# Both filters of the first batch on two queues behind x, in fewer transfers, with the angle work on VectorE

## Chip, cores, metric

The kernel runs on one core of a Trainium2 chip. The metric is the device time of one execution in microseconds (us); lower is better. The profile comes from one execution; its span is about 2 us shorter than the time of the same execution (802.4 against 804.15 us for the kernel before).

Engines are TensorE (PE in the profile, PEld its weight loads), VectorE (DVE), ScalarE (ACT), GpSimd (POOL) and the sync engine (SP). Each of the last three can issue DMA transfers into a queue of its own: in the profile q0 is GpSimd's queue, q1 the sync engine's, q10 ScalarE's. All queues are served by the core's 16 DMA engines.

## The reference

```python
batch, seq, dim = (8, 3008, 256)          # x; filters have seq // 2 + 1 = 1505 rows
X = np.fft.rfft(x, axis=1)
y = np.fft.irfft(X * (filt_r + 1j * filt_i)[None], n=3008, axis=1)
h = y.reshape(24064, 256) @ w_in          # 256 -> 2048
g = h * (1.0 / (1.0 + np.exp(-beta * h)))
out = g @ w_out                           # 2048 -> 256
```

## The kernel before

The transform of length 3008 is cut into 47 x 64 and done as matmuls against tables of sines and cosines. The first batch is transformed alone, since nothing else can run yet: load `x`, first stage (`first1`), turn (`turn_a`), then twelve steps `product(i)` that multiply the spectrum by the real filter and by the imaginary one, each followed by `inverse3`, and a last stage. After it begins the long part, which I call the expert phase: 752 steps (47 blocks of 512 tokens times 16) of the two expert matmuls, among which the other seven batches are transformed. The first matmul of `hps` marks its beginning, and it comes up again and again below as "the first expert matmul".

Both filters live in one tile, `fr_sb`: partitions 0 to 63 hold the real one, 64 to 127 the imaginary one. Each group of a filter takes two transfers, the straight half and a mirrored half whose rows are read backwards.

```python
    def load_x(b, n):
        t = xpool.tile([NP, J, D], BF16, name="xg", tag="xg")
        xv = x[b].rearrange("(p j) d -> p j d", j=J)
        for g in range(n):
            js = slice(g * J // n, (g + 1) * J // n)
            nc.gpsimd.dma_start(t[:80, js, :], xv[:80, js, :])
            nc.gpsimd.dma_start(t[80:NP, js, :], xv[80:NP, js, :])
        return t

    def load_filter(f_sb, filt, at, k0, n, eng, later=False):
        lo = AP(filt.tensor, filt.offset + k0 * D, [[N1 * D, H], [1, n * D]])        # straight
        hi = AP(filt.tensor, filt.offset + (N1 - k0) * D, [[N1 * D, H], [-D, n], [1, D]])  # mirrored
        # ... (one transfer each into f_sb[at:at+H] and f_sb[at+H:at+M])

    # ... (iota, constants)
    x_cur = load_x(0, NJG)                                  # GpSimd's queue
    mark = dpool.tile([1, D], BF16, name="mark", tag="mark")
    nc.sync.dma_start(mark[:], x_cur[:1, 2 * JG, :])        # holds the sync queue until x is there
    for g in range(NG):                                     # NG = 4
        load_filter(fr_sb, filt_r, 0, g * KG, KG, nc.sync)  # real filter
    ws = [load_wout(i * WG, WG) for i in range(2)]          # output weights, sync queue
    # ... keep mask on GpSimd, tables
    angles(0, nc.vector)
    angles(1, gp)                                           # second half of the angles on GpSimd
    for g in range(NG):
        load_filter(fr_sb, filt_i, M, g * KG, KG, gp)       # imaginary filter, GpSimd's queue
    WI = 4
    # ... input weights: WI transfers on GpSimd's queue
    # ... first stage; turn

    for i in range(NK // 2 + 1):
        if i < NK // 2:
            product(i)
        # ... turns, tables, beta
        if i > 0:
            inverse3(i - 1)
    xs[1] = load_x(1, 2)                                    # x of the second batch
```

## Time and profile before

The time before is 803.57 us, the median of 3 runs (802.89 to 804.30).

| Stage of the kernel before | from, to (us) |
|---|---|
| loads, first stage, turn | 0 to 26.2 (first multiply of product 0) |
| product loop (first to last product's multiply) | 26.2 to 43.0 |
| last stage | 43.0 to 48.99 (first expert matmul) |
| expert phase | 48.99 to 802.4 |

The windows view gives the busy time of each engine in a stretch. Its columns are named in its first line; PEclk is the granted clock of TensorE, and a DMA share over 1 means that the records of the engines' packets overlap.

```profile
core 0: us, PE busy (x) PEld busy (x) DVE busy (x) ACT busy (x) POOL busy (x), PEclk, DMA share, GB/s
20.00:30.00 10.00, 5.88 (x49) 4.81 (x48) 4.16 (x8) 4.96 (x10) 3.19 (x6) 0.67 1.07 249
30.00:40.00 10.00, 9.91 (x127) 8.92 (x126) 8.75 (x18) 8.39 (x13) 4.03 (x9) 0.88 1.13 197
...
120.00:780.00 660.00, 658.76 (x5094) 465.76 (x5092) 318.79 (x495) 498.00 (x751) 96.81 (x82) 1.00 0.38 105
```

From 120 us on TensorE is busy 658.8 of 660 us at full clock, so the change has to earn its time before that (or in the last microseconds). There TensorE is idle 4.1 of the 10 us from 20 to 30, and the clock falls to 0.67, while the DMA engines are full.

The timeline shows start, duration, instruction, and in brackets how long the engine sat idle before it and what ended that.

```profile
25.75 0.35 DVE L373 TENSOR_SCALAR fr_sb<-fr_sb,keep 64x256 f32<-64x256 f32 x1 [6.96 <-DMA fr_sb<-in_filt_i_dram]
26.20 0.69 DVE L414 TENSOR_TENSOR pb_t<-ps,fr_sb 128x512 bf16<-128x512 f32 x1
...
43.03 0.68 DVE L414 TENSOR_TENSOR pb_t<-ps,fr_sb 128x512 bf16<-128x512 f32 x1
...
48.99 1.02 PE L735 MATMUL hps<-y,win_sb 128*128 128x512 bf16 x4
```

VectorE waits 6.96 us for the imaginary filter. The chain of waits (start, duration, what) says why that filter is late:

```profile
9.52 1.44 POOL u L257
...
11.04 2.82 POOL r L263
...
13.93 1.80 POOL u L264
...
16.32 9.30 DMA fr_sb<-in_filt_i_dram
```

GpSimd computes its half of the angles (9.5 to 15.7 us) before it issues the imaginary filter, whose second transfer then takes 9.30 us to land.

The third view counts what the queues moved in a window: packets, MB, and the time of those packets as a share of 16 engines. This is the kernel before from 12.5 to 20 us:

```profile
q1 hardware_dynamic: 1165, 1.62, 105.9%
q0 software_dynamic: 3, 0.00, 0.3%
```

A second window of the same kernel, 22 to 28 us, could have been read before predicting too. Both queues have work there, q0 in packets of 4,096 and 6,144 bytes and q1 in packets of 1,024:

```profile
q0 software_dynamic: 315, 1.06, 75.8%
q1 hardware_dynamic: 314, 0.32, 27.8%
```

The numbers of packets are equal and the bytes are not.

### The profile page before, as it was taken

How to read it: one execution, taken by the hardware profiler on the slowest of the kernel's cores; microseconds unless marked ns; L12 is line 12 of the kernel's file. 1: busy time of each engine (PE TensorE's matmuls, PEld its weight loads, DVE VectorE, ACT ScalarE, POOL GpSimd, SP SyncE). 2: the span in 40 equal slices, each digit the busy share in tenths (PEclk: the TensorE clock that was granted, in tenths of full speed). 3: DMA queues.
4: the chain of work that ended last, by engine and by line, in shares of the span. 5: the costliest groups of instructions: out<-in, count | busy, mean ns of one | idle time of the engine just before them, and what ended most of it. 6: DMA issues, size and time to landing. Idle time of an engine off the chain costs nothing.

```text
span 802.4 us, 15376 instructions
## 1 busy us (share of the span) xinstructions
PE 781.1 (97%) x6101; PEld 550.6 (69%) x6101; DVE 411.2 (51%) x665; ACT 588.6 (73%) x896; POOL 154.5 (19%) x157
## 2 busy tenths in 40 slices
PE   6799999999999999999999999999999999999997
PEld 3666667776677666776678766787666776776664
DVE  7676965574627645374653656347462670500101
ACT  4665787787677876788667886678767788677775
POOL 9370520231003400033001410023100240000000
PEclk9799999999999999999999999999999999999999
DMA  8989369322932158211780119602290124110101
GB/s 165 225 180 242 74 163 231 110 93 91 222 120 74 66 140 189 110 48 66 184 228 27 67 56 217 186 27 92 87 243 28 61 79 119 32 54 28 54 27 52
DMA packets 85058, 91.44 MB, mean 114 GB/s; under 512 B 3713, under 2 KB 76178, under 8 KB 84170
## 3 DMA queue, kind: packets, MB, share of 16 engines
q1 hardware_dynamic: 80250, 72.37, 30.5%
q0 software_dynamic: 3072, 14.94, 9.9%
q10 hardware_dynamic: 1664, 3.15, 2.0%
q8 instruction: 47, 0.77, 0.4%
q14 instruction: 25, 0.20, 0.1%
HBM read 57.16 MB, written 46.66 MB: 129 GB/s over the span
## 4 chain that ended last, share of the span: by engine, by line
PE 88%; DVE 4%; DMA 3%; POOL 2%; issue 2%; ACT 1%; DVEq 0%; POOLq 0%; SPq 0%; ACTq 0%
PE acc L763 39%; PE hps L735 38%; PE ps L541 3%; PE ps L489 2%; PE ps L563 2%; PE ps L590 2%; DMA d<-a 1%; DVE ost L775 1%; DMA fr_sb<-in_filt_i_dram 1%; PE psz L424 1%; DVE p_t L573 1%; DVE q_t L577 0%; DVE fi_sb L657 0%; DMA a<-d 0%; PE pz L481 0%
## 5 line engine op out<-in xcount | busy, mean ns | idle before, releaser
L744 ACT ACTIVATE gT<-hps,beta_sb 128x512 bf16<-128x512 f32 x752 | 516.0, 687 | 186.3 <-PE hps L735 173.9
L763 PE MATMUL acc<-wout_sb,gT 128*128 128x256 bf16 x3008 | 455.3, 272 | 2.4 <-DVE ost L775 1.3
L735 PE MATMUL hps<-y,win_sb 128*128 128x512 bf16 (+7 forms) x1728 | 447.6, 351 | 0.0
L763 PEld LDWEIGHTS <-gT 128*128 128x128 bf16 x3008 | 285.7, 98 | 134.2 <-issue 6.2
L735 PEld LDWEIGHTS <-win_sb 128*128 128x128 bf16 x1728 | 164.7, 98 | 24.5 <-issue 0.3
L580 POOL TENSOR_TENSOR v_t<-p_t,q_t 128x512 bf16<-128x512 f32 x84 | 106.6, 1269 | 377.5 <-DVE q_t L577 373.3
L775 DVE COPY ost<-acc 128x512 f32<-128x512 f32 x94 | 60.4, 683 | 193.7 <-PE acc L763 193.7
L107 DVE CAST a<-ps 96x512 bf16<-96x512 f32 x104 | 70.8, 686 | 81.8 <-PE ps L541 81.5
L109 DVE TENSOR_SCALAR y<-ps 128x376 bf16<-128x376 f32 x122 | 66.6, 548 | 65.5 <-PE ps L489 65.2
L573 DVE TENSOR_TENSOR p_t<-ps,fr_sb 128x512 f32<-128x512 f32 x84 | 58.1, 692 | 29.0 <-PE ps L563 27.5
L577 DVE TENSOR_TENSOR q_t<-ps,fi_sb 64x512 f32<-64x512 f32 x84 | 58.3, 694 | 1.2
L574 DVE SCALAR_TENSOR_TENSOR q_t<-ps,fi_sb 64x512 f32<-64x512 f32 x84 | 57.4, 683 | 1.1
L489 PEld LDWEIGHTS <-zz 96*128 96x128 bf16 x512 | 35.5, 98 | 29.1 <-issue 0.2
L105 ACT ACTIVATE z<-ps 128x512 bf16<-128x512 f32 x84 | 49.4, 588 | 1.0 <-PE ps L590 1.0
L541 PE MATMUL ps<-xg,t 94*96 94x512 bf16 x112 | 42.0, 381 | 0.5 <-DVE a L107 0.4
L489 PE MATMUL ps<-t,zz 96*128 96x94 bf16 x448 | 36.8, 205 | 0.0
L590 PE MATMUL ps<-v_t,t 128*128 128x256 bf16 x168 | 32.1, 273 | 0.7 <-DVE q_t L577 0.7
L563 PE MATMUL ps<-a,t 128*128 128x256 bf16 x168 | 32.1, 273 | 0.3 <-DMA a<-d 0.3
L116 POOL DMA_DIRECT2D xg<-in_x_dram x12 | 7.0, 584 | 116.2 <-PE acc L763 97.8
L563 PEld LDWEIGHTS <-t 128*128 128x128 bf16 x168 | 15.8, 98 | 14.8 <-issue 0.4
L541 PEld LDWEIGHTS <-t 94*96 94x96 bf16 x112 | 13.8, 123 | 12.6 <-issue 0.6
L590 PEld LDWEIGHTS <-t 128*128 128x128 bf16 x168 | 15.5, 98 | 8.5 <-DVE q_t L577 1.2
(115 smaller groups left out, 212.5 us busy)
## 6 DMA issues: line engine op xcount, KB each, us to landing
out_dram<-ost SPq DMA_DIRECT2D x41, 512.0 KB, 2.9
d<-a SPq DMA_DIRECT2D x28, 384.0 KB, 7.2
a<-d SPq DMA_DIRECT2D x28, 384.0 KB, 4.4
d<-z SPq DMA_DIRECT2D x28, 384.0 KB, 3.0
zz<-d SPq DMA_DIRECT2D x28, 384.0 KB, 5.1
xg<-in_x_dram POOLq DMA_DIRECT2D x6, 1280.0 KB, 10.2
out_dram<-ost SPq DMA_DIRECT2D x20, 128.0 KB, 3.6
ws<-in_moe_w_out_dram SPq DMA_DIRECT2D x4, 512.0 KB, 17.2
```

The costliest lines, as they stand in the source:

```text
L107: nc.vector.tensor_copy(dst, src)
L109: nc.vector.tensor_scalar_mul(dst, src, scale)
L489: nc.tensor.matmul(ps[:, e, :NP], lhsT=zz[:, jj + e, dc * P : (dc + 1) * P], rhs=tab[:], start=True, stop=True,)
L541: nc.tensor.matmul(ps[:KP], lhsT=t1[:], rhs=s["x"][:, 2 * i : 2 * i + 2, :], start=True, stop=True)
L563: nc.tensor.matmul(ps[:, e, :], lhsT=t2[:, k0 + e, 3:5, :].rearrange("p c k -> p (c k)"), rhs=s["a2"][g][:, kk + e, :], start=True, stop=True,
L573: nc.vector.tensor_tensor(p_t[:], ps[:], fr_sb[:, k0 : k0 + 2, :], ALU.mult)
L580: nc.gpsimd.tensor_tensor(v_t[:], p_t[:], q_t[:], ALU.add)
L590: nc.tensor.matmul(ps[:, e, :], lhsT=t3[:, k0 + e, :], rhs=v_t[:, e, :], start=True, stop=True)
L735: nc.tensor.matmul(hps[:, pos - t0 : pos - t0 + ln], lhsT=win_sb[:, dc, fb * P : (fb + 1) * P], rhs=ys[b][:, dc, n0 : n0 + ln], start=(dc ...
L744: nc.scalar.activation(gT[:, :tn], hps[:, :tn], ACT.Silu, scale=beta_sb[:, fb : fb + 1])
L763: nc.tensor.matmul(acc[tb // 2][:, tb % 2, :], lhsT=gT[:, tb * P : (tb + 1) * P], rhs=wout_sb[:, fb, :], start=(fb == 0 and tb % 2 == 0), ...
L775: nc.vector.tensor_copy(ost[:, 2 * h : 2 * h + n, :], acc[h][:, :n, :])
```

## The change

The intent is to end the 7 us wait. The imaginary filter is issued right behind `x`, before any angle work; both angle halves go to VectorE; each filter comes in three groups instead of four; the input weights and the second batch's `x` follow at once on GpSimd's queue. The inverse runs two products behind instead of one, with a third product buffer, and the second half of the tables is spread over products 0 to 2. In the expert phase some copies go to ScalarE, and the last output copy is shared with it.

```diff
-    apool = pool("apool", 4)
+    apool = pool("apool", 3)
-    pqpool = pool("pqpool", 2)
+    pqpool = pool("pqpool", 3)
...
+    X_WHOLE = [(0, 80, 0, J), (80, NP, 0, J)]
+    X_FIRST = [(0, 80, 0, JG), (80, NP, 0, JG), (0, 80, JG, 2 * JG), (80, NP, JG, J)]
+    X_FIRST += [(0, 80, g * JG, (g + 1) * JG) for g in range(2, NJG)]
...
-    for g in range(NG):
-        load_filter(fr_sb, filt_r, 0, g * KG, KG, nc.sync)
+    FG = ((0, KG), (KG, KG), (2 * KG, 2 * KG))
+    for k0, n in FG:
+        load_filter(fr_sb, filt_r, 0, k0, n, nc.sync)
+    for k0, n in FG:
+        load_filter(fr_sb, filt_i, M, k0, n, gp)
... (keep mask on GpSimd stays here)
+    WI = 2
+    for h in range(WI):
+        fs = slice(h * FF // WI, (h + 1) * FF // WI)
+        gp.dma_start(win_sb[:, :, fs], moe_w_in[:, fs].rearrange("(dc p) f -> p dc f", p=P))
...
-    angles(1, gp)
-    for g in range(NG):
-        load_filter(fr_sb, filt_i, M, g * KG, KG, gp)
-    WI = 4
-    ... (input weights)
+    angles(1, nc.vector)
... (first1 and t2_part reordered; the second table half is spread over products 0 to 2)
+    xs = {}
+    if B > 1:
+        xs[1] = load_x(1, X_WHOLE)              # before the product loop instead of after it
...
-    for i in range(NK // 2 + 1):
+    FLAG = 2
+    for i in range(NK // 2 + FLAG):
...
-        if i > 0:
-            inverse3(i - 1)
+        if i >= FLAG:
+            inverse3(i - FLAG)
...
-        place(1, 15, u1(1), per=2)
+        at = place(1, 11, u1(1, True), per=2)
... (other units placed anew; last output copy and store split between ScalarE and VectorE)
```

More of the change, by code (lines that the diff above doesn't have):

```diff
@@ L109, in evac, with load_x @@
             nc.vector.tensor_scalar_mul(dst, src, scale)
-    def load_x(b, n):
+    def load_x(b, parts):
         t = xpool.tile([NP, J, D], BF16, name="xg", tag="xg")
         xv = x[b].rearrange("(p j) d -> p j d", j=J)
-        for g in range(n):
-            js = slice(g * J // n, (g + 1) * J // n)
-            nc.gpsimd.dma_start(t[:80, js, :], xv[:80, js, :])
-            nc.gpsimd.dma_start(t[80:NP, js, :], xv[80:NP, js, :])
-        return t
+        for p0, p1, j0, j1 in parts:
+            nc.gpsimd.dma_start(t[p0:p1, j0:j1, :], xv[p0:p1, j0:j1, :])
+        return t
+    X_WHOLE = [(0, 80, 0, J), (80, NP, 0, J)]
+    X_FIRST = [(0, 80, 0, JG), (80, NP, 0, JG), (0, 80, JG, 2 * JG), (80, NP, JG, J)]
+    X_FIRST += [(0, 80, g * JG, (g + 1) * JG) for g in range(2, NJG)]
     def load_filter(f_sb, filt, at, k0, n, eng, later=False):
@@ L182 @@
     nc.gpsimd.iota(ic[:], pattern=[[1, P]], base=0, channel_multiplier=0)
-    x_cur = load_x(0, NJG)
+    x_cur = load_x(0, X_FIRST)
     bt = setup.tile([NFB, P], F32, name="bt", tag="bt")
@@ L287 @@
     angles(0, nc.vector)
-    angles(1, gp)
-    for g in range(NG):
-        load_filter(fr_sb, filt_i, M, g * KG, KG, gp)
-    WI = 4
-    for h in range(WI):
-        fs = slice(h * FF // WI, (h + 1) * FF // WI)
-        gp.dma_start(win_sb[:, :, fs], moe_w_in[:, fs].rearrange("(dc p) f -> p dc f", p=P))
+    angles(1, nc.vector)
     a_t = ypool.tile([P, NDC, NK, J, 4], BF16, name="a_t", tag="y")
@@ L321 @@
         warm(2)
-    for part in range(3):
+    t2_part(0, 0)
+    first1(2, (True, True))
+    warm(2)
+    for part in (1, 2):
         t2_part(0, part)
-    for i in range(2, 6):
+    for i in range(3, 5):
         first1(i, (False, False))
@@ L327 @@
     t2_more(0, nc.vector)
-    first1(6, (False, True))
+    first1(5, (True, True))
     warm(2)
-    for part in range(2):
-        t2_part(1, part)
-    first1(7, (False, False))
+    first1(6, (True, True))
+    warm(2)
+    first1(7, (False, True))
+    xs = {}
+    if B > 1:
+        xs[1] = load_x(1, X_WHOLE)
     def table3(i, part, on_act):
@@ L370 @@
     table3(0, 0, True)
-    t2_part(1, 2)
     nc.vector.tensor_scalar_mul(fr_sb[M:P, 0, :], fr_sb[M:P, 0, :], keep[M:P])
@@ L448 @@
             turn_a(2 + 2 * (i // 3) + i % 3, True)
+        if i < 3:
+            t2_part(1, i)
         if i % 3 > 0 and i // 3 < 3:
-            table3(1 + i // 3, 4 - 2 * (i % 3), i % 3 == 1 or i < 3)
-        if i == 2:
+            table3(1 + i // 3, 4 - 2 * (i % 3), i % 3 == 1)
+        if i == 3:
             t2_more(1, nc.vector)
-        if i == 3:
             beta_columns()
@@ L458 @@
             table4()
-        if i > 0:
-            inverse3(i - 1)
-    xs = {}
-    if B > 1:
-        xs[1] = load_x(1, 2)
+        if i >= FLAG:
+            inverse3(i - FLAG)
     for i in range(4):
@@ L629, in place @@
             last_at = at
+        return last_at
     def u1(b, act=False):
@@ L665, in go @@
         def go():
-            xs[b] = load_x(b, 1)
+            xs[b] = load_x(b, X_WHOLE)
         return [go]
-    place(1, 13, uz(1))
-    place(1, 9, uf(), per=2)
+    place(2, 14, uz(1, True))
     place(15, 29, uz(2))
-    place(34, 60, uz(3, True))
+    place(34, 58, uz(3, True))
     first_step = [(S * b // TB) * NFB for b in range(B + 1)]
     if B > 1:
-        place(1, 15, u1(1), per=2)
-        place(20, 20, [lambda: a2_read(1)], per=9)
-        place(26, 56, u23(1), per=2)
-        place(60, 60, [lambda: zz_read(1)], per=9)
+        at = place(1, 11, u1(1, True), per=2)
+        place(at + 1, at + 1, [lambda: a2_read(1)], per=9)
+        place(1, 9, uf(), per=9)
+        at = place(22, 54, u23(1), per=2)
+        assert at < 58
+        place(58, 58, [lambda: zz_read(1)], per=9)
         place(66, 78, u4(1), per=2)
@@ L683 @@
         place(36, 36, ux(2), per=9)
-        place(50, 66, u1(2, True), per=3)
+        at = place(50, 66, u1(2, True), per=3)
+        assert at < 74
         place(74, 74, [lambda: a2_read(2)], per=9)
@@ L694, with store @@
         place(a + 63, a + 78, u4(b))
-    def store(t0, tn, ost):
+    def store(t0, tn, ost, eng=nc.sync):
         if t0 >= S:
-            nc.sync.dma_start(
+            eng.dma_start(
                 out[t0 : t0 + tn, :].rearrange("(c p) d -> p c d", p=P), ost[:, : tn // P, :]
@@ L774 @@
                     n = min(2, nch - 2 * h)
-                    nc.vector.tensor_copy(ost[:, 2 * h : 2 * h + n, :], acc[h][:, :n, :])
-                store(t0, tn, ost)
+                    last = i == NBLK - 1
+                    evac(
+                        ost[:, 2 * h : 2 * h + n, :], acc[h][:, :n, :], h == 0 and (i < 6 or last)
+                    )
+                    if last:
+                        store(t0 + 2 * h * P, n * P, ost[:, 2 * h :, :], (nc.scalar, nc.sync)[h])
+                if not last:
+                    store(t0, tn, ost)
 _INS = ['x', 'filt_r', 'filt_i', 'moe_w_in', 'moe_w_out', 'moe_beta']
```

## The prediction

> **What bounds the kernel.** By the windows view TensorE is busy 99 to 100% from 120 to 780 us at full granted clock; two 128x512 and four 128x256 matmuls make a step of 0.87 us. The change leaves that work alone, so three places can move: the start before the first expert matmul (at 48.99 us in the timeline), stalls up to 120 us, and the tail.
>
> Start. The timeline shows x landing up to 13.4 us, the first product's matmuls at 19.44, and VectorE idle 6.96 us until 25.75 for the filter, so the first product is multiplied at 26.2. The chain of waits leads back to GpSimd: its half of the angles (1.44 + 2.82 + 1.80 us, 9.5 to 15.7) stands before the issue of the imaginary filter, whose second transfer takes 9.30 us to land. From 26.2 to 44.3 VectorE is nearly saturated (24 multiplies of 0.68 us = 16.5, plus copies). The granted clock falls to 0.50 at 19 to 22 and 26 to 32 us, after idle stretches; the Trainium skill, "TensorE: Matmul & The Clock Gate", Part 1, describes this half clock, and the trace agrees (256-column pairs take 0.63 instead of 0.38 us).
>
> **What the change does.**
> - The imaginary filter is queued right behind x, before any angles. DMA is already about 100% busy from 4 to 43 us, and the skill ("Trainium Kernel Development and Optimization", Key Constraints) says that all queues share 16 engines: order is gained, not bandwidth. From the 230 to 250 GB/s of 12 to 26 us I estimate both first groups landed by 16 to 18 us, all by 27; the merged last group is needed only at product 6.
> - Angles on VectorE add 1.01 + 0.56 + 0.96 = 2.5 us there, at 9 to 11.5 us, where it can wait; three casts (0.48 each) go to ScalarE. The copy that took 1.97 us beside GpSimd should take 0.35.
> - The second table half (0.84 + 0.83 + 1.25 us of ScalarE) goes into products 0 to 2; one more table copy (0.55) goes to VectorE. The later inverse and third product buffer should hide this.
>
> **Sum.** First multiply at 18.0 to 19.5 instead of 26.2: about -7. The product loop becomes 19.6 us of VectorE work plus 1.5 to 2 of waits instead of 18.1: +2.5 to 3. Sharing stage copies and output copies with ScalarE removes perhaps 0.5 to 1 of about 3 us of TensorE idleness at 49 to 120 us, though ScalarE gets tight in the first 11 steps. In the tail the second 0.65 us output copy runs beside the first: -0.65. First expert matmul at about 44 us; total -5 to -7.
>
> **Predicted: 797.0 us, 8 in 10 between 793.5 and 801.0.** Chances: faster by over 2% 0.02, within 2% 0.97, slower by over 2% 0.01.
>
> **Right if** the timeline has the first product's multiply before 20 us, no wait of VectorE for the imaginary filter over 1.5 us, the first expert matmul at 42.5 to 45.5, and the span after that matmul shorter by 0.5 to 2 us.
>
> **Wrong if** the filter's landing still holds the first product (the output weights ride behind the real filter on the same engines): then 800 to 802. If TensorE stays at full clock and ScalarE keeps up, the loop costs nothing extra: 793 to 795. If ScalarE (by my count about 18 us of work in the loop) becomes the bound, or x of the second batch lands after 44 us, 2 to 3 us are given back. Against my main step speaks that DMA is full: a transfer issued earlier only displaces others.

## The result and the profile after

The changed kernel takes 808.63 us, the median of 4 runs (808.35 to 809.15), beside 803.61 us for the kernel before (802.89 to 804.30, 4 runs). The ratio is 1.0063, 95% interval 1.0046 to 1.0081. Ratios in this document are the mean time of one kernel's runs over that of the kernel before in the same rounds, so they are not quite the ratio of the medians quoted beside them. The kernel became slower by 5 us where 6.6 us of gain were predicted. (The two executions that the profiles show took 804.15 and 808.35 us, so 4.2 us of the 5.0 are to be found in them.)

The same three views, for the kernel after. First the windows:

```profile
20.00:30.00 10.00, 5.74 (x53) 5.08 (x53) 6.97 (x15) 4.97 (x9) 0.59 (x3) 0.66 1.13 235
30.00:40.00 10.00, 4.99 (x72) 4.51 (x70) 2.42 (x5) 5.69 (x9) 0.34 (x2) 0.95 1.02 213
40.00:50.00 10.00, 7.64 (x76) 6.49 (x76) 7.80 (x14) 3.85 (x8) 7.24 (x8) 0.70 0.26 80
120.00:780.00 660.00, 658.77 (x5091) 465.57 (x5090) 318.22 (x494) 499.93 (x755) 96.68 (x82) 1.00 0.38 106
```

The stretch from 120 to 780 us is as it was. From 30 to 40 us TensorE now works 4.99 us instead of 9.91, and from 40 to 50 us its clock is 0.70 while the DMA share has dropped to 0.26: the data came late, and then the engines had nothing left to move.

The timeline:

```profile
16.12 0.35 DVE L383 TENSOR_SCALAR fr_sb<-fr_sb,keep 64x256 f32<-64x256 f32 x1
...
22.92 0.69 DVE L424 TENSOR_TENSOR pb_t<-ps,fr_sb 128x512 bf16<-128x512 f32 x1 [6.45 <-DMA fr_sb<-in_filt_r_dram]
...
39.87 0.69 DVE L424 TENSOR_TENSOR pb_t<-ps,fr_sb 128x512 bf16<-128x512 f32 x1 [7.32 <-DMA fr_sb<-in_filt_r_dram]
...
47.24 0.68 DVE L424 TENSOR_TENSOR pb_t<-ps,fr_sb 128x512 bf16<-128x512 f32 x1
...
53.19 1.02 PE L747 MATMUL hps<-y,win_sb 128*128 128x512 bf16 x4
```

The imaginary filter did what the change wanted: the instruction at 16.12 us, which needs it, waits for nothing, where it waited 6.96 us before. But VectorE now waits twice for the **real** filter, 6.45 us before product 0 and 7.32 us before product 6. The chain of waits has one long link, the last transfer of the real filter, issued at 13.37 us and landed 26.38 us later:

```profile
13.37 26.38 DMA fr_sb<-in_filt_r_dram
...
40.48 0.69 DVE qb_t L424
...
53.19 1.02 PE hps L747 x4
```

The gains and losses up to the first expert matmul add up exactly, from the two timelines: first multiply 26.20 to 22.92 (-3.28); product loop, first to last product, 16.83 to 24.32 (+7.49, of which 7.32 are the wait before product 6); last product to first expert matmul 5.96 to 5.95. The sum is +4.20, from 48.99 to 53.19. The expert phase gives back 0.35 (753.38 to 753.03). The span grew by 3.8 us.

Why is a transfer of the real filter under way for 26 us, when the DMA engines move over 200 GB/s? The queue view shows two things. From 11.5 to 16 us, just after the real filter was issued on q1, only q0 is served:

```profile
q0 software_dynamic: 221, 0.99, 104.7%
```

And from 29 to 33.5 us, with the second batch's `x` on q0 and the rest of the real filter on q1:

```profile
q0 software_dynamic: 62, 0.97, 103.3%
q1 hardware_dynamic: 56, 0.06, 5.5%
```

The two queues moved nearly the same **number** of packets, 62 and 56, but q0's are of 16,384 bytes and q1's of 1,024 (the mirrored half of the filter: one row of 256 floats each). So q0 got 0.97 MB and 103% of the engines' time, and q1 0.06 MB. At 56 packets per 4.5 us, q1's 1,024-byte rows crawl until `x` is in.

### The profile page after: what moved, and what is told of

It is laid out like the page before. It is cut to its first block, busy times and chain, and to the rows that moved or that the text cites. A ratio compares the mean times of both kernels' runs of the same rounds, so it can differ in the third digit from the quotient of the medians.

```text
span 806.2 us, 15374 instructions
## 1 busy us (share of the span) xinstructions
PE 780.4 (97%) x6101; PEld 550.8 (68%) x6101; DVE 398.7 (49%) x644; ACT 599.1 (74%) x920; POOL 142.2 (18%) x146
## 4 chain that ended last, share of the span: by engine, by line
PE 88%; DMA 5%; DVE 3%; issue 2%; ACT 1%; POOL 0%; SPq 0%; ACTq 0%; DVEq 0%; POOLq 0%
PE acc L775 39%; PE hps L747 38%; DMA fr_sb<-in_filt_r_dram 3%; PE ps L550 3%; PE ps L498 2%; PE ps L572 2%; PE ps L599 2%; DVE ost L107 1%; DMA d<-a 1%; DMA xg<-in_x_dram 1%; DVE p_t L582 0%; ACT gT L756 0%; DMA a<-d 0%; DVE q_t L583 0%; DVE q_t L586 0%
## 5 line engine op out<-in xcount | busy, mean ns | idle before, releaser
L107 DVE COPY ost<-acc 128x512 f32<-128x512 f32 x87 | 56.1, 683 | 195.7 <-PE acc L775 189.1
L107 DVE CAST a<-ps 96x512 bf16<-96x512 f32 x96 | 65.9, 686 | 84.4 <-PE ps L550 82.8
L109 DVE TENSOR_SCALAR y<-ps 128x376 bf16<-128x376 f32 x118 | 64.4, 548 | 61.6 <-PE ps L498 61.4
L115 POOL DMA_DIRECT2D xg<-in_x_dram x20 | 10.9, 550 | 121.2 <-PE acc L775 97.7
## 6 DMA issues: line engine op xcount, KB each, us to landing
d<-a SPq DMA_DIRECT2D x28, 384.0 KB, 11.1
xg<-in_x_dram POOLq DMA_DIRECT2D x7, 1280.0 KB, 10.4
```

Source lines behind the costliest of these rows:

```text
L107: nc.vector.tensor_copy(dst, src)
L109: nc.vector.tensor_scalar_mul(dst, src, scale)
```

## The experiments

The theory, which I call **S**: while two queues both have work, they get about equal numbers of packets whatever their size, so a queue of small packets starves beside one of large packets. The Trainium skill has the ground for it in "DMA: Bandwidth & Descriptors", section "Queues, rings and completion order": each engine goes round the queues that have work, at the granularity of a packet. It takes a packet for a bundle of descriptors; that turns are equal in the packets which the profile counts is what the traces here show. With S comes an observation, **L**: a queue that joins while the other keeps the engines full gets nothing for some time, 5 to 6 us in the kernels before and after (what the length of this gap follows is said under "What stays open"). The rivals were: only the bytes queued ahead count (order and volume, not packets); the merged last group alone is to blame; or the cost sits in the schedule (the later inverse, ScalarE), not in the DMA.

Landing times are the ends of the transfers in the trace, or, where a transfer has no end on record, the time at which the instruction that waited for it went on. The edits are against the kernel named in their first line.

### E1: the second x after the real filter (e1_x_gated)

```diff
# against the kernel after
+    gate = dpool.tile([2, D], F32, name="gate", tag="gate")
+    gp.dma_start(gate[:], fr_sb[H - 1 : H + 1, NK - 1, :])   # reads the real filter's last rows
     xs = {}
     if B > 1:
         xs[1] = load_x(1, X_WHOLE)
```

> Changed kernel, but the load of the second batch's x waits until the last real-filter transfer has landed. Theory S (the queues take turns packet by packet, so the 1 KB packets of the real filter on the sync queue are starved by the GpSimd queue's packets of 2 KB (input weights) and 16 KB (second x)): the last real-filter transfer lands at 29 to 31 us instead of 39.8, the second VectorE wait (7.3 us) disappears, the first (6.45 us) stays; 801 to 802.5 us. Rival B (the DMA is simply full until 40 us, so the last bytes are late whatever the order): the second wait keeps at least 4 us; about 806 or more. Rival M (only the merged last group is late): second wait also stays.

Measured: 808.59 us, ratio 1.0065 (1.0050 to 1.0080). The total missed. The second wait for the filter is gone, as S says (the gate let go at 32.7 us, where I had expected the filter at 29 to 31), but a wait of TensorE took its place, seen in the waits view (engine, line, releaser: us in total, times, longest):

```profile
PE bps L392 <- POOL id_f L391: 6.4, 1, 6.4
```

GpSimd stood at the gate until the filter had landed, and the small identity matrix `id_f`, which it makes later and which beta's transpose needs, came late. This is a fault of the experiment; E9 repeats it cleanly.

### E9: the same, without the fault (e9_x_gated_clean)

```diff
# against E1: GpSimd makes id_f ahead of the gate
+    id_f = setup.tile([NFB, NFB], F32, name="id_f", tag="id_f")
+    gp.tensor_copy(id_f[:], ident[:NFB, :NFB])
     gate = dpool.tile([2, D], F32, name="gate", tag="gate")
...
     def beta_columns():
-        id_f = setup.tile(...)
-        gp.tensor_copy(id_f[:], ident[:NFB, :NFB])
```

> Changed kernel with the second x held back behind the real filter, as in e1, but with GpSimd's 16x16 identity copy ahead of that hold, so that TensorE's transpose of beta (which waited 6.4 us for it in e1) is free. S: the real filter lands near 32.5 us as in e1, so the wait at product 6 shrinks from 7.3 us to 0 to 1.5; the first wait (6.5 us) stays; second x lands at 43 to 44.5 us, just ahead of its use; first expert matmul at 46 to 47.5 us; 801 to 803 us. Rival B: 806 or more.

Measured: 801.31 us, ratio 0.9970 (0.9954 to 0.9987), so 7.3 us under the kernel after. From its timeline:

```profile
23.10 0.69 DVE L426 TENSOR_TENSOR pb_t<-ps,fr_sb 128x512 bf16<-128x512 f32 x1 [6.64 <-DMA fr_sb<-in_filt_r_dram]
...
45.71 1.02 PE L749 MATMUL hps<-y,win_sb 128*128 128x512 bf16 x4
```

The first wait stays (6.64 us), the second is gone, and the first expert matmul comes 7.5 us earlier than after (45.71 against 53.19), about the size of the second wait, 7.32. So the early second `x` causes the whole second wait, and the wait is worth its full length in the total. By itself this run does not tell packets from bytes, since the gate moves both; E3 does.

### E2: input weights and x after the real filter (e2_both_gated)

```diff
# against the kernel after: the same gate, ahead of the input weights
+    gate = dpool.tile([2, D], F32, name="gate", tag="gate")
+    gp.dma_start(gate[:], fr_sb[H - 1 : H + 1, NK - 1, :])
     WI = 2
     for h in range(WI):
```

> Changed kernel, but the input weights and then the second x wait until the last real-filter transfer has landed. Theory S: nothing but the imaginary filter and, late, the output weights shares the engines with the real filter; first groups landed by 17.5 us, both VectorE waits for the real filter under 1 us, first expert matmul at 40 to 42.5 us instead of 53.2, perhaps 1 us lost on the second x at the first steps; 796 to 799 us. Rival B: the sum of the waits stays above 6 us or turns up at the input weights; 803 or more.

Measured: 806.20 us, ratio 1.0034 (1.0019 to 1.0049), a miss. The second wait is gone and the whole real filter is in by 28.7 us, but a first wait of 4.5 us remains, with nothing but `x` and the imaginary filter ahead of it. So the input weights explain at most 2 of the first wait's 6.45 us (E4 below has a first wait of 4.6 us with the input weights in place). The fault of E1 is in this kernel too (a wait of 6.8 us of TensorE), so its total says little.

### E3: the second x in small packets (e3_small_packets)

```diff
# against the kernel after: same place, same bytes, in four transfers instead of two, 2,048-byte instead of 16,384-byte packets
-        xs[1] = load_x(1, X_WHOLE)
+        tv = t.rearrange("p (c b r) d -> p b c (r d)", b=2, r=4)
+        xv = x[1].rearrange("(p c b r) d -> p b c (r d)", c=J // 8, b=2, r=4)
+        for p0, p1 in ((0, 80), (80, NP)):
+            for b in range(2):
+                gp.dma_start(tv[p0:p1, b], xv[p0:p1, b])
```

> Changed kernel, second x loaded just as early and in the same place of its queue, but by a pattern that makes its packets 2 KB instead of 16 KB written. Theory S: the real filter gets about an eighth as many foreign bytes per packet of its own; its last transfer lands at 31 to 33 us instead of 39.8, the second VectorE wait falls from 7.3 us to under 1.5, the first stays at 6.45; 801.5 to 803 us. Rival B, and any theory that counts bytes or order of issue only: no change, 808.6.

Measured: 804.97 us, ratio 1.0008 (0.9991 to 1.0025). The queue view of this kernel in the same window as above:

```profile
q0 software_dynamic: 326, 0.63, 76.2%
q1 hardware_dynamic: 327, 0.32, 37.0%
```

And its timeline:

```profile
36.45 0.69 DVE L430 TENSOR_TENSOR pb_t<-ps,fr_sb 128x512 bf16<-128x512 f32 x1 [3.08 <-DMA fr_sb<-in_filt_r_dram]
```

Packets are equal again, 326 and 327, and q1 moves 0.32 MB instead of 0.06 in the same 4.5 us. Bytes ahead and order of issue are as in the kernel after, so for the second wait the rival that only these count is refuted. The second wait fell from 7.32 to 3.08 us, where I had expected under 1.5: with 2,048 against 1,024 bytes the filter still gets under half of the engines' time (37.0%), which I had counted too generously. The first multiply came 1.4 us later than in the kernel after (24.29 us), and the total stayed 2 us above the expected 801.5 to 803.

### E4: four filter groups instead of three (e4_four_groups)

```diff
# against the kernel after
-    FG = ((0, KG), (KG, KG), (2 * KG, 2 * KG))
+    FG = tuple((g * KG, KG) for g in range(NG))
```

> Changed kernel with the filters in four equal groups again instead of two and a double one. Rival M (the merge made the second wait): the wait at the seventh product disappears and does not come back; about 801.5 us. Theory S: the third group is there for product 6, but the fourth still lands at about 39.8 us behind the second x, so the wait moves to product 9 and shrinks to 2 to 4 us; 804 to 806 us. The first wait stays at about 6.4 us in both.

Measured: 804.01 us, ratio 1.0004 (0.9986 to 1.0022). The second wait moved from product 6 to product 9 and still lasts 5.1 us, until 39.2 us; the first is 4.6 us. The merged group makes the wait begin sooner, but it is not its cause: without it, the last rows of the filter land at about the same time (39.2 against 39.9 us). In the total, though, the merge is nearly the whole loss: this kernel is 4.6 us under the kernel after and level with the kernel before. Three products stand behind the last landing instead of six, and the first group is in 2.0 us earlier (first multiply 20.88 us, where I had expected no change; the input weights are issued 2.2 us later here, at 14.58 us). So it took both, the late landing and the merged group, to lose the 5 us.

### E8: the real filter in long rows (e8_long_rows)

```diff
# against the kernel after: the mirrored half is read forwards, so its packets are 6 or 12 KB (a wrong result)
-    for k0, n in FG:
-        load_filter(fr_sb, filt_r, 0, k0, n, nc.sync)
+    for k0, n in FG:
+        for at, first in ((0, k0), (H, N1 - k0 - n + 1)):
+            rows = AP(filt_r.tensor, filt_r.offset + first * D, [[N1 * D, H], [1, n * D]])
+            nc.sync.dma_start(fr_sb[at : at + H, k0 : k0 + n, :].rearrange("p k d -> p (k d)"), rows)
```

> Changed kernel, wrong result on purpose: the mirrored half of the real filter is read unmirrored, so that its rows are 6 and 12 KB packets instead of 1 KB; the same rows, bytes, queues and order of issue. S with L: the lag until about 16 us stays, then the real filter takes most of the bytes; first group by 18.5, all by 25; the first wait shrinks from 6.45 us to 1 to 2.5, the second disappears; 797 to 799.5 us. Rival B or any theory of bytes or order alone: 808.6 as the changed kernel.

Measured: 806.44 us, ratio 1.0036 (1.0012 to 1.0059); the result is wrong by intent. The start did what S says. Its queues from 18 to 23 us:

```profile
q1 hardware_dynamic: 189, 0.87, 68.1%
q0 software_dynamic: 180, 0.39, 37.7%
```

Equal packets again (189 and 180), but now the filter's packets are the larger ones and q1 moves 0.87 MB against 0.39. The second wait is gone, the first is 4.7 us, and the first expert matmul comes at 42.82 us, 10.4 us earlier than after. The total missed by 7 us, for a reason of the same kind:

```profile
DVE a L107 <- DMA d<-a: 8.4, 1, 8.4
```

The output weights, in 1,024-byte packets behind the filter on q1, were now the ones that met the second `x` and its 16,384-byte packets; they landed at about 41 us, their second half was issued only at 45.6 and 50.7 us, and a store of the expert phase that stands behind them on the same queue came 8.4 us late. From 31 to 36 us q0 moved 69 packets and q1 67 in this kernel, 1.04 MB against 0.07: the starvation had only found another victim.

### E11: the real filter at once (e11_no_mark)

```diff
# against the kernel after
-    mark = dpool.tile([1, D], BF16, name="mark", tag="mark")
-    nc.sync.dma_start(mark[:], x_cur[:1, 2 * JG, :])
```

> Changed kernel without the copy that holds the real filter back until 10.8 us: the real filter is issued at 1 us on an empty queue. L: it gets packets at once (by 3 us, no lag) and shares the engines with the first x, packet by packet; all of it has landed by 18 us, the first x only at 15 to 18 us instead of 12.1; first multiply at 19 to 22 us, then no wait for the real filter; 797 to 801 us. If the lag belongs to the sync queue itself and not to joining a full one, its first packets come 4 to 5 us after issue here too.

Measured: 802.68 us, ratio 0.9989 (0.9975 to 1.0003). The real filter is issued at 1.2 us, and from 2 to 3.5 us it is already served:

```profile
q1 hardware_dynamic: 120, 0.26, 74.6%
q0 software_dynamic: 2, 0.01, 4.5%
```

So the sync queue itself starts promptly; the gap of 5 us is seen only where a queue joins a full other one. No product waits for the real filter any more. But now the first `x` takes turns with it and lands at 17.6 us instead of 12.1, and the first multiply comes at 23.3 us, no earlier than before this edit (19 to 22 expected). The total missed the expected 797 to 801 us because I had not counted what the filter takes from `x`.

### E5 and E6: one part of the change each, on the kernel before (e5_filter_early, e6_angles_only)

```diff
# E5, against the kernel before: filter first, angles still on GpSimd
+    for g in range(NG):
+        load_filter(fr_sb, filt_i, M, g * KG, KG, gp)
     WG = NFB // 4
...
     angles(1, gp)
-    for g in range(NG):
-        load_filter(fr_sb, filt_i, M, g * KG, KG, gp)
```

> Kernel before with one edit: the imaginary filter's eight transfers are issued right behind x, ahead of GpSimd's half of the angles. After the first four runs the theory S has a second part, L: a queue whose transfers are issued while the other queue is full gets no packet for about 5 us (real filter issued at 11.1, first packets at 15.5 to 17 in the changed kernel; imaginary filter issued at 15.7, first packets at 21.5 before). S with L: real filter's first group lands near 20.5 us, GpSimd's angles end near 18.5 and hold ScalarE and so the first product until about 22; nothing later starves, because the second x is still issued after 33 us; no second wait; 799.5 to 801.5 us. Rival (the early filter itself is the loss): 804 or more.

Measured: 803.31 us, ratio 0.9992 (0.9967 to 1.0016). A miss: two waits came in place of the one. The real filter is waited for 3.6 us, and ScalarE waits for GpSimd's angles, which now come after the filter's eight issues:

```profile
ACT t L275 <- POOL u L267: 7.5, 1, 7.5
```

```diff
# E6, against the kernel before: one word
-    angles(1, gp)
+    angles(1, nc.vector)
```

> Kernel before with one edit: both halves of the angles on VectorE. The imaginary filter is then issued from about 9.5 us without being moved in the program. S with L: the real filter joins a full queue, its first group lands at 20 to 21 us, first multiply there instead of at 26.2, VectorE's 2.5 us of angles partly delay the first casts; 799 to 801 us. Rival (VectorE's extra work is what costs): 804 or more.

Measured: 798.77 us, ratio 0.9938 (0.9911 to 0.9964). The timeline of E6:

```profile
19.35 0.69 DVE L414 TENSOR_TENSOR pb_t<-ps,fr_sb 128x512 bf16<-128x512 f32 x1 [0.42 <-PE ps L405]
...
42.66 1.02 PE L735 MATMUL hps<-y,win_sb 128*128 128x512 bf16 x4
```

With only this word changed, the first multiply comes at 19.35 us (26.20 before) and the first expert matmul at 42.66 (48.99 before). The order of the queues is kept: the real filter joins at 10.0 us when little of `x` is left, its first group is in at 13.7, the imaginary filter's at 16.4, and the second `x` is issued at 28.0 us, after all filters. This part of the change alone has 4.8 of the 6.6 us that were predicted; the moved transfers lost them again, as E7 confirms, which keeps all the rest of the change.

### E7: both filters on one queue (e7_one_queue)

```diff
# against the kernel after: the filters alternate by group on GpSimd's queue
     for k0, n in FG:
-        load_filter(fr_sb, filt_r, 0, k0, n, nc.sync)
-    for k0, n in FG:
+        load_filter(fr_sb, filt_r, 0, k0, n, gp)
         load_filter(fr_sb, filt_i, M, k0, n, gp)
```

> Changed kernel with both filters on the GpSimd queue, group by group, behind x; the sync queue holds only the output weights. S with L: within one queue the order is kept, both first groups have landed by 16 to 17 us, the first multiply is at 17.5 to 18.5; output weights of 1 KB packets on the other queue slow the last (double) group, landing at 28 to 30, a wait of 0 to 3 us at product 6; 797 to 800.5 us. Rival B (DMA full, order does not matter): waits of 8 us or more in sum, 804 or more.

Measured: 798.63 us, ratio 0.9943 (0.9919 to 0.9967), as expected. All transfers of the kernel after are there, in the same sizes, and the second `x` is still early; the queue of the real filter is another, and with it its time of issue: on GpSimd's queue the `mark` no longer holds it, so it is issued from 5.6 us on instead of 11.1. First multiply at 18.1 us, first expert matmul at 42.57. The total is 10.0 us under the kernel after. Not all of that is the queue: E11 has the early issue on a queue of its own and takes 802.68 us, so about 6 of the 10 us come with an early issue alone and about 4 are left to the shared queue, as far as two kernels can be subtracted. VectorE still waits 2.9 us for the imaginary filter at product 6, while the output weights on q1 take turns with it.

### E10: one queue, four groups, keep mask first (e10_one_queue_four)

```diff
# against E7: four groups in turn, the keep mask ahead of the filters, x of batch 2 used later
-    FG = ((0, KG), (KG, KG), (2 * KG, 2 * KG))
-    for k0, n in FG:
-        ... (both filters)
     ... (keep mask)
+    for g in range(NG):
+        load_filter(fr_sb, filt_r, 0, g * KG, KG, gp)
+        load_filter(fr_sb, filt_i, M, g * KG, KG, gp)
...
-        at = place(1, 11, u1(1, True), per=2)
+        at = place(4, 14, u1(1, True), per=2)
```

> Candidate for the best: both filters on the GpSimd queue in four groups each, real and imaginary in turn, the keep mask computed before they are issued (it cost 1.9 us of VectorE's time in e7), and the first stage of the second batch from step 4 instead of step 1, since its x lands near 44 us. S: first multiply at 16.2 to 17.2 us, no wait for a filter over 1 us, first expert matmul at 39.3 to 41 us (42.57 in e7), up to 1.5 us given back on the second x; 795.5 to 797.5 us. If DMA volume binds after all: 798 to 799, as e7, with the gain given back at the second x.

Measured: 802.03 us, ratio 0.9977 (0.9961 to 0.9993), 4.5 us above the range. The issue itself became the limit. In the trace the k-th transfer that GpSimd issues waits for the landing of the transfer eight before it (in the kernel before, the first issue of the input weights comes at 23.66 us, just after the transfer eight before it landed at 23.37). With sixteen filter transfers GpSimd was held until about 27 us, and TensorE then waited 3.8 us for `id_f`, which GpSimd makes afterwards. For a queue that carries both filters, fewer and larger transfers were a good part of the change.

### E12: everything on one queue in the order of need (e12_all_one_queue)

```diff
# against E7
-    for k0, n in FG:
-        ... (both filters)
+    both_filters(*FG[0])
     ... (keep mask; id_f made here)
+    for k0, n in FG[1:]:
+        both_filters(k0, n)
+    ws = [load_wout(i * WG, WG, gp) for i in range(2)]       # was the sync queue
     ... (input weights, then the second x, as in E7)
```

> From e7 (both filters alternating on GpSimd's queue) with three moves: the keep mask and the 16x16 identity are computed between the issues of the first filter group and of the later ones, and the first two output-weight transfers go on the same queue, after the filters and before the input weights, so that no second queue takes turns with the filters. Equal packet turns predict: first multiply at 16.5 to 18 us instead of 18.1; filters all landed by 26 to 28 us instead of 29.8, because the roughly 900 packets of output weights that went by before that no longer come between; no VectorE wait for a filter over 1.5 us (2.9 in e7); the first expert matmul at 40.5 to 41.5 us instead of 42.57; median 796.0 to 798.0. The view that only the bytes in front of a filter count predicts the same landing within 1 us for the filters' last group (the output weights are under 1 MB of the 6 that move by then) and 798 to 799. What would spoil it: GpSimd's issue blocked by its 8 rotating semaphores, which would let the second x land after 46 us and put a wait into the expert phase.

Measured: 799.17 us, ratio 0.9939 (0.9926 to 0.9953). The start came as expected: first multiply at 16.7 us, first expert matmul at 41.35 (42.57 in E7). The longest wait that the view puts down to a filter is 0.6 us; before product 6, though, VectorE sat idle for 1.71 us and went on at 28.84, just after the last filter transfer had landed at 28.55, so the filter was waited for there too. I had expected that landing at 26 to 28; it is 1.2 us earlier than in E7 (29.78), where a count of bytes alone allowed under 1, so E12 does not tell the two apart. The total is above the expected 796 to 798 and no better than E7's, and the timeline shows where the 1.2 us went:

```profile
45.02 0.63 PE L555 MATMUL ps<-xg,t 94*96 94x512 bf16 x2 [2.65 <-DMA xg<-in_x_dram]
```

TensorE waits 2.65 us for the second batch's `x`, which lands at 45.0 us. The DMA engines are full from 4 to 45 us in this kernel, so an earlier product loop only reaches the end of the queue sooner.

### E13 and E14: the second x used three steps later (e13_one_queue_x_later, e14_two_queues_x_later)

```diff
# E13 against E12, and E14 against E7
-        at = place(1, 11, u1(1, True), per=2)
+        at = place(4, 14, u1(1, True), per=2)
```

> e12 with one number changed: the second batch's first stage starts at step 4 of the expert phase (place 4 to 14) instead of step 1 (1 to 11). In e12 the first expert matmul came at 41.35 us, but TensorE then waited 2.7 us for the second x, which landed at 45.0, and the stretch from the first expert matmul to the end was 755.6 us instead of e7's 753.5. If the engines of the DMA are the bound of the start by now, so that what an earlier product loop gains is handed back at x, then a later use of x gets it: wait for x under 0.5 us, first expert matmul still 41.0 to 41.7, stretch to the end 752.5 to 754, median 796.5 to 798.0. The rival, that the 2 us are lost elsewhere in the expert phase (ScalarE, buffers), expects the stretch still at 755 or more and a median of 798.5 to 799.5.

> e7 with the same one number changed (second batch's first stage at steps 4 to 14). In e7 x landed at 43.9 us and the first expert matmul came at 42.6, so the wait for x was small: if the wait for x is what costs, little changes here (median 798.0 to 799.0, within 0.6 us of e7); if a later start of the second batch's first stage is better for another reason (ScalarE or VectorE too full in the first steps), e7 gains about as much as e12 does, 1 to 2 us.

Measured: E13 takes 797.20 us, ratio 0.9921 (0.9909 to 0.9933), and has the lowest median (its interval overlaps those of E6, E7, E12 and E14); E14 takes 798.62, ratio 0.9942 (0.9928 to 0.9955), the same as E7. In E13 the matmul that waited before now waits for nothing:

```profile
40.65 1.02 PE L752 MATMUL hps<-y,win_sb 128*128 128x512 bf16 x4
...
45.14 0.38 PE L555 MATMUL ps<-xg,t 94*96 94x512 bf16 x1
```

The stretch from the first expert matmul to the end went from 755.7 us in E12 to 754.2 in E13 (just over the 752.5 to 754 expected), and from 753.5 in E7 to 753.3 in E14. So the wait for `x` was most of what E12 gave back, 1.5 of its 2.2 us over E7. The remaining 0.9 us of E13 over E14 in that stretch is not explained by a run; E13's trace has a wait of TensorE of 1.5 us that E14's has not, for a copy on VectorE that had itself waited 3.2 us for a store. And of the 2.0 us between the medians of E12 and E13, 0.7 lie in an earlier start (40.65 against 41.35) that the edit does not cause; the two intervals just overlap.

| Kernel | first multiply | first expert matmul | first expert matmul to end | median |
|---|---|---|---|---|
| before | 26.2 | 48.99 | 753.4 | 803.6 |
| after | 22.9 | 53.19 | 753.0 | 808.6 |
| E9: second x gated | 23.1 | 45.71 | 753.4 | 801.3 |
| E6: before, one word | 19.4 | 42.66 | 754.5 | 798.8 |
| E7: one filter queue | 18.1 | 42.57 | 753.5 | 798.6 |
| E12: all on one queue | 16.7 | 41.35 | 755.7 | 799.2 |
| E13: E12, x used later | 16.6 | 40.65 | 754.2 | 797.2 |

All times are in us; the last column is the median of the runs, the others are from the one profiled execution.

## Why the prediction was wrong

**The step that failed** is, in the words of the prediction: "The imaginary filter is queued right behind x, before any angles ... I estimate both first groups landed by 16 to 18 us, all by 27". It divided bytes by a rate, as if both queues were one line served in order. ("Order is gained" was the prediction's own conclusion, not the cited page's.) The imaginary filter did land by 14.0 us (first group) and 20.1 us (all). The real filter landed its first group at 22.9 and its last at 39.9 us. Two things held it. It was issued at 11.1 us while the other queue kept the engines full, and got nothing until 16.5 us (L; 221 packets on q0 and none on q1 from 11.5 to 16). And from then on it took turns packet by packet with input weights of 2,048 and `x` of 16,384 bytes, with half of its own bytes in packets of 1,024 (S). The prediction never asked in which queue the bystanders were: it watched the filter that was moved, and not the transfers that the move brought forward against the other one. The merged last group, "needed only at product 6" in the prediction, then put six products behind the latest landing instead of three (E4: 4.6 us).

**The objection that I wrote down and under-weighed.** "DMA is full: a transfer issued earlier only displaces others" was right, and the "wrong if" case of 800 to 802 us still too low by 7, since I took displacement to cost as many bytes as were moved. E3 shows that the size of the packets, and not the bytes alone, set the price: with the same bytes in the same place the total fell from 808.6 to 805.0 us. That case also named the wrong neighbour: the output weights stand behind the filter on its own queue, and what competes with it in the trace is on the other one.

**The size of the loop.** The prediction allowed 2.5 to 3 us more for the product loop. Without the wait before product 6 it takes 24.32 - 7.32 = 17.0 us against 16.83 before, so +0.2. ScalarE did not become a bound here, where it could work ahead during the first wait. In E13, where the loop begins at 16.6 us, the loop takes 18.1 us and ScalarE is busy 7.45 of the 8 us from 20 to 28; there the term measures +1.3, with ScalarE as its likely cause. The later inverse and the third buffer did what they were meant to, or were not needed; no run takes them away alone.

**The expert phase and the tail.** Predicted -0.5 to -2, measured -0.35 (753.38 to 753.03), which one pair of profiles does not resolve from nothing: runs of one kernel differ by as much. In the tail the second copy does run beside the first, but the second half of the accumulator is ready 0.22 us after the first, and that copy ends 2.34 us after the last group of matmuls begins, where it was 2.72. To the end of the span it is 6.43 us instead of 6.63, so -0.2 instead of -0.65.

**What was right.** The moved filter no longer held anything; the angles fit on VectorE (E6: 798.77 us with nothing else changed); the clock halves after idle stretches, which the Trainium skill describes in "TensorE: Matmul & The Clock Gate", Part 1: the granted clock was 0.50 from 22.5 to 28 us and again from 40 to 45 us in the kernel after, each time after a wait for the filter, and 1.00 in E6 in both stretches. And 797 us could be had: E13 reaches 797.20 with the same angles and the same transfers of the filters, but by another way: on one queue, with the output weights on it too and the second `x` used later.

**What stays open.** Why a joining queue gets nothing at first. Equal turns alone would not give it, and no run isolates its mechanism. The traces show that the gap is not a constant: it follows what the other queue has been issued and has not moved yet. From the issue of the `mark` copy to the first packet on q1 it is 1.3 us in E6, 3.1 in E12, 5.3 in E7 and 5.7 in the kernel after, and q0 moves 0.24, 0.68, 1.26 and 1.30 MB in it. By the sizes of the transfers in the code I estimate that 0.25, 0.71, 1.27 and 1.57 MB had been issued there and not moved when q1 joined. So for a queue that joins, the bytes ahead do seem to count, most of them; in the kernel before the joining q0 waited from 15.7 to 21.5 us in the same way.

## What to carry to other kernels

Before moving a transfer forward on full DMA engines, list what every queue will hold at that time with its packet size: a queue of 1 KB rows beside one of 16 KB rows gets a sixteenth of the other's bytes, so urgent transfers of short rows belong on the same queue as the large ones, ahead of them in the order of need. What has already been issued on the other queue when yours joins goes first for the most part. Issue what is not urgent late enough that it can't meet what is, and keep transfers few where the issuing engine also computes, but do not merge rows that are needed early with rows that are needed late: everything then waits for the last of them (E4). When an early part has been gained, look at what it now waits for next: here the gain past 42 us was handed back at the next full-queue load until its use was moved too.

## What the Trainium skill lacked or had wrong

- "Trainium Kernel Development and Optimization", Key Constraints, says that issuing from several engines "only saves the sequencer's issue time". It says nothing of what the choice does to the order of landing. Putting the real filter on the other queue, with the earlier issue that came with it, is worth 10.0 us of 808.6 (E7), some 4 of them beyond an early issue alone (E11), and the queues take turns by packets (62 against 56, with 0.97 against 0.06 MB).
- "DMA: Bandwidth & Descriptors", "Queues, rings and completion order", states the turns by packet, and the windows shown here in which both queues had work agree (315 and 314; 62 and 56; 326 and 327; 189 and 180). It does not draw the consequence, that bandwidth is then shared in proportion to packet size and a queue of short rows starves.
- The same page, "SWDGE vs HWDGE vs iDMA", gives 4,096 bytes as the preferred bound of a packet. The records that the profile counts as packets reach 16,384 bytes on GpSimd's queue here (1.23 us each on one engine), and the turns are taken by these.
- No page has the gap before a queue that joins full engines is served at all: 961 packets on q1 and none on q0 from 15.7 to 21.0 us in the kernel before, although the transfer on q0 was issued at 15.68. It is 1.3 us with 0.24 MB ahead (E6) and 5.7 us with 1.30 MB ahead (after).
